# Attention and two expert layers: separate names for shared memory, merged loads, a fourth output buffer, a new table of order

## The chip, the cores and the metric

The kernel runs on one core of one Trainium2 chip. The metric is the device time of one execution in microseconds (us), the median of the runs shown. Three runs of the kernel before gave 1088.44, 1091.89 and 1093.85 us.

## The reference

Everything is float32. Attention has 4 batches of 8 heads, 576 positions and 64 channels; then come two pairs of dense layers (2304 tokens, 512 channels, 2048 hidden).

```python
scores = q @ k.T / 8                       # per batch and head, 576 x 576
keep   = scores >= max(scores, -1) - tau   # the others are set to -1e9
attn   = exp(scores - max); attn /= sum(attn) + 1e-9
x      = (attn @ v) laid out as (batch*seq, heads*64)
h = x @ w_in;  g = s * relu(h)**2 + b;  x = g @ w_out          # first layer pair
h = x @ w_in2; g = max(h,0) + alpha * min(h,0); out = g @ w_out2   # second pair
```

The weights arrive as 8-byte numbers and are turned into 4-byte ones on the chip.

## The kernel before

**How the order is made.** The kernel first lists about 6,800 tasks (`plan.add`): an engine, a time in us that the author gives, the buffers read and written, a rank. `Plan.run` (L696) then plays them in a simulated clock: whenever an engine is free it takes the ready task of the lowest rank whose buffers are open, and in that moment the task's instructions are issued. So the order in each engine's queue is fixed when the kernel is built; on the chip every engine works through its queue in that order and waits by semaphores where data is late. `MOVES` is a table that adds a number to the rank of task n; it is the order "written out". In the old planner a DMA costs SP 0.6 us and ends a fixed time later (`LAND` plus its kilobytes over 180, and `BUSY` added for some).

**Stages.** (1) The first batch's four head pairs ("whole" pairs): k and q are loaded, transposed by TensorE, scores are made (L1311) and reduced to a maximum (DVE L1321), exponentials are taken (ACT L1325), cut and summed (DVE L1327), transposed back by TensorE (`turned_e`, lines L848 and L850), copied out of PSUM by ACT (L1439) into tiles called exponentials here, and multiplied with v (L1451, a burst of 20 matmuls). (2) The other three batches do the same in a split form (L1471), and in the gaps the first layer pair ("MoE A", L1057 to L1059) runs on the columns that are done. (3) The rest of the first pair, from 480 us on. (4) The second pair, from 745 us on, which multiplies 2x2 blocks with seven products.

**Memory that the change touches.** `gt` is one large tile, placed at a fixed address under two names of type (`g32`/`gt`, L898). Its first part, ten slots, takes the first block's features (`g0_s`, written by ACT L1098 and POOL or DVE L1099). The rest is cut into slices that serve as exponentials of the first batch (`of_e`, L1145, shown in the profile as `gt`); later the whole tile holds other features.

**Transposes.** One transpose task turns 1 to 4 blocks; `flip` (L846) makes all but the last in a one-pass type (L848) and the last in plain float32 (L850).

**Outputs of stage 3.** Each block of 384 tokens gives four results; ACT (L1705) or DVE (L1714) writes each into a buffer of `yb_s` (three, L1605) and SP sends it to memory (L1707, L1717). `sm_s` (four buffers) holds block sums of the second pair's weights (`seven`, `weights`).

**Loads.** Each head pair's k, q and v come in one DMA per head (L1184, 128 KB each, rows of 64 channels), the last 64 positions in small ones (L1203, L1198). SP issues nearly all DMAs; the k and q splits go through SBUF copies (`hk`, `hq`, L1267 and L1271).

**Warm matmuls.** `warm` (L1407) is a 128x128 matmul whose result nobody reads: 12 at the start, a few behind the first pair's transposes and its first two scores (`FILL`, `FILLS`, `FILL1`).

Of the kernel before, what the change touches and what calls it, by code (L numbers as in the profile page):

```python
# [17 lines left out]
P = 128  # L18
# [13 lines left out]
FILL, FILL1 = 12, 3  # L32
# [5 lines left out]
BUSY = 180  # L38
# [620 lines left out]


class Task:
    __slots__ = ("ways", "engine", "fn", "bufs", "needs", "next", "tail", "port")


class Plan:
    HOP = 0.2
    SELF = {"ACT": 0.12, "DVE": 0.12, "POOL": 0.06}
    LAND = 2.0

    def __init__(self):  # L670
        self.tasks = []
# [1263 lines left out]
```

## Time and profile before

| what | value |
|---|---|
| median of 3 runs | 1091.89 us |
| the profiled execution | 1095.99 us |
| its span, first to last instruction | 1094.2 us |
| TensorE matmul busy (PE) | 1058.2 us (97%) |
| VectorE (DVE), ScalarE (ACT), GpSimd (POOL) busy | 873.7, 702.4, 351.3 us |
| mean granted TensorE clock | 0.988 |
| chain that ended last | PE 83%, DVE 5%, DMA 4%, ACT 4%, issue 2% |

The span leaves 1.8 us of the execution around it. The chain is followed back from the last instruction, at each step to what released it. Lines such as L1439 are those of the kernel before; the lines of a helper (L848, L1057) stand for all its callers.

### The profile page before, as it was taken

How to read it: one execution, taken by the hardware profiler on the slowest of the kernel's cores; microseconds unless marked ns; L12 is line 12 of the kernel's file. 1: busy time of each engine (PE TensorE's matmuls, PEld its weight loads, DVE VectorE, ACT ScalarE, POOL GpSimd, SP SyncE). 2: the span in 40 equal slices, each digit the busy share in tenths (PEclk: the TensorE clock that was granted, in tenths of full speed). 3: DMA queues.
4: the chain of work that ended last, by engine and by line, in shares of the span. 5: the costliest groups of instructions: out<-in, count | busy, mean ns of one | idle time of the engine just before them, and what ended most of it. 6: DMA issues, size and time to landing. Idle time of an engine off the chain costs nothing.

```text
span 1094.2 us, 21344 instructions
## 1 busy us (share of the span) xinstructions
PE 1058.2 (97%) x7074; PEld 1003.8 (92%) x7074; DVE 873.7 (80%) x1976; ACT 702.4 (64%) x1649; POOL 351.3 (32%) x494
## 2 busy tenths in 40 slices
PE   8788899999999999999989999999999999999998
PEld 7556699989898988999989999999999999999998
DVE  6787888987888888847766787578999999998882
ACT  5897878886987788753543264465656876655551
POOL 2576645653764467520000012020102334112110
PEclk9898999999999999999999999999999999999999
DMA  5763465565455554426475576337786564554531
GB/s 130 208 189 121 120 159 136 122 168 144 109 126 137 145 142 108 131 68 189 118 231 163 184 263 206 109 111 242 263 255 212 171 211 142 153 158 118 147 99 39
DMA packets 195183, 170.90 MB, mean 156 GB/s; under 512 B 73216, under 2 KB 173568, under 8 KB 195072
## 3 DMA queue, kind: packets, MB, share of 16 engines
q1 hardware_dynamic: 191888, 167.11, 53.6%
q10 hardware_dynamic: 3184, 2.43, 0.8%
q8 instruction: 55, 0.90, 0.3%
q14 instruction: 56, 0.46, 0.1%
HBM read 98.97 MB, written 49.28 MB: 135 GB/s over the span
## 4 chain that ended last, share of the span: by engine, by line
PE 83%; DVE 5%; DMA 4%; ACT 4%; issue 2%; POOL 1%; SPq 1%; DVEq 0%; ACTq 0%; POOLq 0%
PE bank L1057 13%; PE bank L1058 13%; PE bank L1059 13%; PE bank_b L1058 9%; PE bank_b L1057 9%; PE bank_b L1059 9%; PE sc L1311 7%; PE bank L1471 5%; PE bank L850 3%; PE bank L848 3%; DVE e L1327 1%; PE bank L1451 1%; DMA stg<-in_moe_w_in_dram 1%; DMA yf<-yb 1%; ACT e L1325 1%
## 5 line engine op out<-in xcount | busy, mean ns | idle before, releaser
L1327 DVE SCALAR_TENSOR_TENSOR e<-sc,mx,e 128x576 f32<-128x576 f32 x144 | 116.5, 812 | 16.8 <-ACT e L1325 13.1
L1321 DVE TENSOR_REDUCE mx<-sc 128x1 f32<-128x576 f32 x144 | 107.3, 751 | 19.5 <-PE sc L1311 18.1
L1325 ACT ACTIVATE e<-sc,mx 128x576 f32<-128x576 f32 x144 | 106.7, 744 | 9.5 <-DVE mx L1321 8.9
L850 PE MATMUL bank<-eyes_r,e 128*128 128x128 f32 (+1 forms) x320 | 89.5, 292 | 0.9 <-DVE e L1327 0.9
L1057 PE MATMUL bank<-xt,wa 128*128 128x480 f32 (+3 forms) x224 | 82.4, 368 | 0.8 <-ACT rest L1088 0.7
L1057 PE MATMUL bank<-gt0r,wa 128*128 128x384 f32 (+4 forms) x214 | 75.7, 354 | 2.1 <-ACT rest L1088 1.9
L1323 POOL TENSOR_SCALAR mx<-mx,tau_s 128x1 f32<-128x1 f32 x144 | 49.3, 343 | 83.6 <-DVE mx L1321 73.8
L1058 PE MATMUL bank<-xt,wa 128*128 128x480 f32 (+3 forms) x224 | 76.1, 340 | 0.0
L1059 PE MATMUL bank<-xt,wa 128*128 128x480 f32 (+3 forms) x224 | 76.0, 339 | 0.0
L1058 PE MATMUL bank<-gt0r,wa 128*128 128x384 f32 (+4 forms) x214 | 72.1, 337 | 0.0
L1059 PE MATMUL bank<-gt0r,wa 128*128 128x384 f32 (+4 forms) x214 | 72.0, 337 | 0.0
L1471 PE MATMUL bank<-gl,vt 128*128 128x256 f32 (+1 forms) x192 | 65.0, 340 | 0.2 <-POOL gl L1504 0.2
L1471 PE MATMUL bank<-gh,vt 128*128 128x256 f32 (+1 forms) x192 | 57.7, 301 | 0.0
L1035 POOL TENSOR_TENSOR wa<-stg,wa 128x256 fp32r<-128x256 f32 x9 | 7.1, 789 | 147.9 <-ACT wa L1034 147.9
L1509 DVE TENSOR_TENSOR gl<-bank,gh 128x256 fp32r<-128x256 f32 (+1 forms) x96 | 43.5, 453 | 12.7 <-ACT gh L1507 11.7
L1311 PE MATMUL sc<-k,q 128*128 128x288 f32 x200 | 47.5, 361 | 5.5 <-DMA k<-hk 2.9
L1507 ACT ACTIVATE gh<-bank 128x256 fp32r<-128x256 f32 (+1 forms) x96 | 39.7, 413 | 19.2 <-PE bank L850 18.1
L1519 POOL TENSOR_TENSOR gr<-gf,gh 64x256 fp32r<-64x256 f32 (+1 forms) x48 | 38.5, 801 | 40.8 <-DVE gl L1517 26.8
L850 PEld LDWEIGHTS bank<-eyes_r,e 128*128 128x128 f32 (+1 forms) x320 | 45.2, 141 | 5.3 <-DVE e L1327 1.3
L1057 PEld LDWEIGHTS bank<-xt,wa 128*128 128x128 f32 x224 | 43.5, 194 | 3.3 <-ACT rest L1088 1.6
L951 DVE SCALAR_TENSOR_TENSOR n<-stg,n 128x512 int32<-128x512 int32 x64 | 44.5, 696 | 1.0
L1504 POOL TENSOR_TENSOR gl<-gf,gh 128x256 fp32r<-128x256 f32 (+1 forms) x48 | 38.7, 806 | 20.2 <-ACT gh L1502 13.1
(697 smaller groups left out, 4140.9 us busy)
## 6 DMA issues: line engine op xcount, KB each, us to landing
stg<-in_moe_w_in_dram SPq DMA_DIRECT2D x32, 512.0 KB, 4.1
stg<-in_moe_w_out_dram SPq DMA_DIRECT2D x32, 512.0 KB, 3.9
gf<-gw SPq DMA_DIRECT2D x44, 192.0 KB, 3.0
gw<-gf SPq DMA_DIRECT2D x52, 128.0 KB, 2.9
q<-hq SPq DMA_DIRECT2D x24, 256.0 KB, 4.7
qo<-hq SPq DMA_DIRECT2D x24, 256.0 KB, 4.3
xt<-xs SPq DMA_DIRECT2D x14, 384.0 KB, 4.5
yf<-yb SPq DMA_DIRECT2D x24, 192.0 KB, 2.6
```

Of the source, the lines that this page charges most:

```text
L850: nc.tensor.transpose(to, part(x), one)
L951: add("DVE", dve(DM), lambda: nc.vector.scalar_tensor_tensor(ni(), word(0), 29, ni(), op0=ALU.logical_shift_right, op1=ALU.bitwise_or), (n ...
L1057: nc.tensor.matmul(o, lhsT=wl, rhs=mh, start=first, stop=False, skip_group_check=on_top)
L1058: nc.tensor.matmul(o, lhsT=wh, rhs=ml, start=False, stop=False, skip_group_check=on_top)
L1059: nc.tensor.matmul(o, lhsT=wh, rhs=mh, start=False, stop=last, skip_group_check=on_top)
L1311: nc.tensor.matmul(sp.t[:, x, :HS], lhsT=o[0][:, c], rhs=o[1][:, x * HS:(x + 1) * HS], start=n == 0, stop=n == len(passes) - 1)
L1321: add("DVE", dve(S), lambda sp=sp, mx=mx: nc.vector.tensor_reduce(mx.t[:, 0:1], sp.t[:, :, :HS], op=ALU.max, axis=AX.XY, negate=True), (sp ...
L1323: t2 = add("POOL", 0.26, lambda mx=mx: nc.gpsimd.tensor_scalar(mx.t[:, 1:2], mx.t[:, 0:1], -1.0, tau_s, op0=ALU.mult, op1=ALU.subtract), ( ...
L1325: add("ACT", act(S, 1), lambda sp=sp, mx=mx, e=e: nc.scalar.activation(halves(e.t), sp.t[:, :, :HS], AF.Exp, bias=mx.t[:, 0:1]), (sp, mx), ...
L1327: add("DVE", dve(S) + 0.065, lambda sp=sp, mx=mx, e=e, col=col, sums=sums: nc.vector.scalar_tensor_tensor(halves(e.t), sp.t[:, :, :HS], mx ...
L1471: nc.tensor.matmul(o.t[:, :n], lhsT=w.rearrange("p a b -> p (a b)"), rhs=m.t[:, :n], start=c == first and x == 0, stop=c == last and x == ...
L1509: add("DVE", dve(n), lambda hi=hi, lo=lo, gt=gt: nc.vector.tensor_tensor(lo.t[:, :n], gt.t[:, :n], f32(hi.t[:, :n]), op=ALU.subtract), (gt ...
```

## The change

- `gt` (later features), `g0` (the first block's features) and `ge0`, `ge1`, ... (the exponentials' slices) become separately named tensors at the same addresses as before.
- k and q of a head pair are loaded by one DMA each, with both heads; v too, and v's tile is laid out head by head, so that a head's four blocks of a position are one run of 1024 bytes.
- `yb_s` gets four buffers, `sm_s` three.
- Two warm matmuls follow every score of the first batch but those that had three (`FILL2`).
- The last block of a transpose task is also turned in the one-pass type where the planner saw the next TensorE task begin at once and both are transposes (`joined`). For this the planner issues a TensorE task only when the next one starts.
- The planner's costs are new: a DMA takes SP 0.5 us (0.65 or 1.0 for some), all DMAs share one simulated line, and transposes cost other times. `MOVES` is a new table for the new numbers of the tasks (68 more warm ones, 48 fewer loads).

```diff
-FILL, FILL1 = 12, 3
+FILL, FILL1, FILL2 = 12, 3, 2
...
 MOVES = {
-    0: -28.8, 1: -4.97, 2: 0.748, 3: 7.76, 4: -3.45, 5: -0.433, 6: 2.58, 7: -22.4, 8: -31.3, 9: -41.5, 10: -32.9, 11: -14.1, 12: -51.2, 13: -49.6,
...
+                        if e == "PE":
+                            joined = t.turn and freed == (now, True)
+                            us -= self.JOIN * joined
+                            release(joined)
+                            held_back, freed = t, (None, t.turn)
...
+                        end = now + us
+                        if t.load:
+                            end = line = max(line, end + self.SEND) + t.load
+                        at(end + t.tail, "end", t)
...
     def turned(k):
-        return 0.109 + (0.06 + 0.085 * (k - 2) if k > 1 else 0.0)
+        return 0.112 + 0.061 * (k - 1)
...
     def flip(to, x, part, i, n, one, one_r):
-        if i < n - 1:
+        if i < n - 1 or plan.joined:
             nc.tensor.transpose(to.bitcast(F32R), part(as_r[id(x)]), one_r)
...
-    g32 = placed(1, "gt", [P, (NA - 3) * 2 * TA])[0]
-    gt = as_r[id(g32)]
+    def at(name, n, dt, o):
+        return nc.alloc_sbuf_tensor_at(name, [P, n], dt, offset=o).ap()
+
+    ng, n0 = (NA - 3) * 2 * TA, NA * 2 * FIRST[0][1]
+    end[0] -= 4 * ng
+    gt, g0 = at("gt", ng, F32R, end[0]), at("g0", n0, F32R, end[0])
+    ge = [at(f"ge{i}", G2, F32, end[0] + 4 * (n0 + i * G2)) for i in range((ng - n0) // G2)]
...
-    def hwdge(fn, reads=(), writes=(), rank=None, kb=128, after=()):
-        return add("SP", 0.6, fn, reads, writes, after, rank, tail=Plan.LAND + kb / 180.0)
+    def carried(kb, part):
+        return 1.4 * kb * 1024 / part * (0.0083 + 0.0369e-3 * part) / 16
+
+    def hwdge(fn, reads=(), writes=(), rank=None, kb=192, after=(), part=1536, far=0.0, us=0.5):
+        return add("SP", us, fn, reads, writes, after, rank, tail=far, load=carried(kb, part))
...
-                for h in range(2):
-                    def load(t=t, src=src, h=h):
-                        nc.sync.dma_start(
-                            t.t[:, 0:NQ, h, :], src[b, h0 + h, 0:NQ * P, :].rearrange("(p c) d -> p c d", c=NQ))
-
-                    hwdge(load, (), (t,), base - 12 * STEP, 128 + BUSY * (p > 0))
+                if nm == "v":
+                    hwdge(lambda t=t, src=src: nc.sync.dma_start(
+                        t.t.rearrange("p c h d -> p (c h d)").rearrange("p (h x) -> p h x", h=2)[:, :, :NQ * D], src[b, h0:h0 + 2, 0:NQ * P, :].rearrange("h (p c) d -> p h (c d)", c=NQ)),
+                        (), (t,), base - 12 * STEP, 256, (), 1024, 0.4)
+                    continue
+                hwdge(lambda t=t, src=src: nc.sync.dma_start(
+                    t.t[:, :NQ], src[b, h0:h0 + 2, 0:NQ * P, :].rearrange("h (p c) d -> p c h d", c=NQ)),
+                    (), (t,), base - 12 * STEP, 256, (), 256, 0.4, 1.0)
...
-                        for _ in range(FILL1 if p == 0 and i < 2 else 0):
+                        for _ in range((FILL1 if p == 0 and i < 2 else FILL2) if base < NP * 4 * STEP else 0):
                             warm(LATER, plan.tasks[-1:])
...
-            for slots, n, name, shape in ((ya_s, 2, "yat", [P, TB]), (yb_s, 3, "yb", [P, TB]),
-                                          (sm_s, 4, "sm", [P, G1])):
+            for slots, n, name, shape in ((ya_s, 2, "yat", [P, TB]), (yb_s, 4, "yb", [P, TB]),
+                                          (sm_s, 3, "sm", [P, G1])):
```

## Rows read from the trace of the kernel before

**Rows 1.** Busy time by stage: window, length, each engine's busy us, PEclk, DMA

```profile
0.00:150.00 150.00, 129.53 (x841) 101.28 (x841) 117.48 (x256) 113.06 (x254) 85.36 (x127) 0.94 0.56 152
150.00:480.00 330.00, 323.48 (x2325) 300.99 (x2324) 276.36 (x645) 265.31 (x616) 185.46 (x278) 0.99 0.53 131
480.00:600.00 120.00, 115.64 (x636) 113.27 (x635) 75.50 (x139) 47.31 (x93) 1.89 (x2) 0.97 0.54 168
600.00:1075.00 475.00, 474.85 (x3159) 473.81 (x3158) 401.77 (x931) 275.94 (x687) 78.59 (x87) 1.00 0.58 177
```

**Rows 2.** PE's waits: waited for, us in total, times, longest

```profile
PE sc L1311 <- DVE e L1327: 4.3, 6, 2.4
PE bank L848 <- ACT e L1325: 3.4, 1, 3.4
PE sc L1311 <- DMA k<-hk: 2.9, 1, 2.9
PE bank_b L1057 <- ACT gt0r L1109: 2.6, 1, 2.6
PE bank L1057 <- ACT rest L1088: 2.6, 3, 1.9
```

**Rows 3.** Four stretches in which the granted clock was 0.50, columns as in Rows 1

```profile
33.40:40.20 6.80, 6.08 (x23) 4.71 (x24) 5.10 (x11) 4.39 (x11) 3.01 (x4) 0.50 0.65 199
101.60:108.40 6.80, 6.33 (x31) 5.57 (x30) 4.42 (x9) 4.72 (x11) 3.80 (x5) 0.50 0.40 125
139.20:142.60 3.40, 3.40 (x19) 3.40 (x18) 3.27 (x5) 2.71 (x8) 3.40 (x5) 0.50 0.37 117
569.30:576.10 6.80, 5.93 (x17) 5.53 (x18) 4.03 (x8) 1.73 (x4) 0.00 (x0) 0.50 0.71 218
```

**Rows 4.** A wait of ACT from 95 to 150 us, columns as in Rows 2

```profile
ACT gt0r L1098 <- PE bank L1451: 6.7, 3, 2.8
```

**Rows 5.** The chain from 95 to 150 us: start us, us, what

```profile
94.76 1.64 PE bank L1451 x12
...
96.48 0.42 ACT gt0r L1098
...
99.49 0.75 DVE e L1327 x2
```

**Rows 6.** A wait of ACT, in the whole span, columns as in Rows 2

```profile
ACT yb L1705 <- DMA yf<-yb: 4.6, 1, 4.6
```

**Rows 7.** The chain from 555 to 572 us

```profile
559.11 8.23 DMA yf<-yb
```

**Rows 8.** PE in order of time: start us, us, line, operands

```profile
14.56 0.30 PE L850 MATMUL bank<-eyes_r,nat 128*128 128x128 f32 x1
...
334.65 0.23 PE L848 MATMUL bank<-eyes_r,e4r 128*128 128x128 f32 x1
334.71 0.30 PE L850 MATMUL bank<-eyes_r,e 128*128 128x128 f32 x1
...
334.97 0.28 PE L1471 MATMUL bank<-gh,vt 128*128 128x256 f32 x1
335.09 0.23 PE L848 MATMUL bank<-eyes_r,e5r 128*128 128x128 f32 x1
...
479.50 0.30 PE L850 MATMUL bank<-eyes_r,e 128*128 128x128 f32 x1
```

**Rows 9.** DMA issues: operands, queue, count, KB each, median us to landing

```profile
stg<-in_moe_w_in_dram SPq DMA_DIRECT2D x32, 512.0 KB, 4.1
...
nat<-in_k_dram SPq DMA_DIRECT2D x32, 128.0 KB, 3.2
...
nat<-in_v_dram SPq DMA_DIRECT2D x24, 32.0 KB, 2.5
```

**Rows 10.** SP's time for one load's issue, L1184: min/median/max ns

```profile
L1184 SPq DMA_DIRECT2D nat<-in_k_dram x32: 543/604/1697, 0.7 to 413.2; - x32
```

**Rows 11.** Ten warm matmuls in a row at full clock, columns as in Rows 8

```profile
11.53 1.28 PE L1409 MATMUL bank<-eyes_r 128*128 128x128 f32 x10
```

More of the change, by code (lines that the diff above doesn't have):

```diff
@@ L37 @@
 AT_ONCE = 4
-BUSY = 180
 LAG = 2
@@ L661 @@
 class Task:
-    __slots__ = ("ways", "engine", "fn", "bufs", "needs", "next", "tail", "port")
+    __slots__ = ("ways", "engine", "fn", "bufs", "needs", "next", "tail", "port", "load", "turn")
 class Plan:
@@ L667, with add @@
     SELF = {"ACT": 0.12, "DVE": 0.12, "POOL": 0.06}
-    LAND = 2.0
+    SEND = 1.0
+    JOIN = 0.05
     def __init__(self):
-        self.tasks = []
-    def add(self, engine, us, fn, reads=(), writes=(), after=(), rank=None, tail=0.0, port=False):
+        self.tasks, self.joined = [], False
+    def add(self, engine, us, fn, reads=(), writes=(), after=(), rank=None, tail=0.0, port=False, load=0.0, turn=False):
         t = Task()
-        t.fn, t.next, t.tail, t.engine, t.port = fn, [], tail, None, port
+        t.fn, t.next, t.tail, t.engine, t.port, t.load, t.turn = fn, [], tail, None, port, load, turn
         n = len(self.tasks)
@@ L699, in run @@
         busy = dict.fromkeys(engines, False)
-        port = None
-        events, n, left = [], 0, len(self.tasks)
+        port = held_back = None
+        events, n, left, line, freed = [], 0, len(self.tasks), 0.0, (None, False)
         def at(time, kind, x):
@@ L710, in offer, with go, release @@
                 heapq.heappush(ready[e], (rank, t, us))
+        def go(t, e):
+            if len(t.ways) > 1:
+                t.fn(e)
+            else:
+                t.fn()
+        def release(joined):
+            nonlocal held_back
+            if held_back is not None:
+                self.joined = joined
+                go(held_back, "PE")
+                held_back = None
         for t in self.tasks:
@@ L735, in run @@
                         t.engine = e
-                        if len(t.ways) > 1:
-                            t.fn(e)
+                        if e == "PE":
[3 more added lines that the diff above has]
+                            held_back, freed = t, (None, t.turn)
                         else:
-                            t.fn()
+                            go(t, e)
                         busy[e] = True
                         at(now + us, "free", e)
-                        at(now + us + t.tail, "end", t)
+                        end = now + us
+                        if t.load:
+                            end = line = max(line, end + self.SEND) + t.load
+                        at(end + t.tail, "end", t)
                         break
@@ L752, in run @@
                     port = None
+                if x == "PE":
+                    freed = now, freed[1]
             elif kind == "end":
+                if x is held_back:
+                    release(False)
                 left -= 1
@@ L945, in mult @@
                 on(e).tensor_scalar(n32.t, f32(word(1)), REBIAS, None, op0=ALU.mult)
-        hwdge(load, (), (raw, *also), rank, 512, after)
+        hwdge(load, (), (raw, *also), rank, 512, after, 1024 if inner else 4096, 0.4)
         add([("DVE", 0.34, rank), ("ACT", act(DM, 0, True) + 0.04, rank)], 0, mult, (raw,), (n32,), port=True)
@@ L1043, in whole @@
         numbers(src, kind == "i", f, raw, n32, rank, after)
-        hwdge(lambda: nc.sync.dma_start(wf[kind][f * P:(f + 1) * P, :], n32.t), (n32,), (wf_d[kind][f],), rank, 262)
+        hwdge(lambda: nc.sync.dma_start(wf[kind][f * P:(f + 1) * P, :], n32.t), (n32,), (wf_d[kind][f],), rank, 256, (), 2048)
     def weights(kind, u, rank, after):
@@ L1050, in weights @@
             raw.t.rearrange("p (h n) -> p h n", h=2), wf[kind].rearrange("(h u p) n -> u p h n", h=2, p=P)[u]),
-            [wf_d[kind][u], wf_d[kind][u + NF // 2]], (raw,), rank, 524, after)
+            [wf_d[kind][u], wf_d[kind][u + NF // 2]], (raw,), rank, 512, after, 2048, 0.3)
         q = {f"{i + 1}{j + 1}": (raw, lambda o=(2 * i + j) * G1: raw.t[:, o:o + G1]) for i in range(2) for j in range(2)}
@@ L1068, in load_x @@
             t = hwdge(lambda x=x, c=c: nc.sync.dma_start(
-                f32(x.t[:, :, :n]), src[:, c * P:(c + 1) * P, c0:c0 + n].rearrange("a p t -> p a t")), bufs[c], (x,), rank, 1.024 * n, chain[0])
+                f32(x.t[:, :, :n]), src[:, c * P:(c + 1) * P, c0:c0 + n].rearrange("a p t -> p a t")), bufs[c], (x,), rank, n, chain[0], 4 * n, 0.6)
             xs.append(x)
@@ L1143, in attention @@
         v32, o = tiles(ep, NP, "v32", [P, NK, 2, D]), NS * P
-        f0 = NA * 2 * FIRST[0][1]
-        of_e = gf + sh + tiles(ep, 1, "gp", [P, G2]) + [g32[:, i:i + G2] for i in range(f0, g32.shape[1] - G2 + 1, G2)]
+        of_e = gf + sh + tiles(ep, 1, "gp", [P, G2]) + ge
         for t in of_e:
@@ L1165, in halves, with by_head @@
             return t.rearrange("p (a b) -> p a b", a=2)
+        def by_head(t):
+            return t.t.rearrange("p c h d -> p (c h d)").rearrange("p (h c d) -> p h c d", h=2, d=D)
         def half(h):
@@ L1181, in pair @@
                 t = nat[nm] = Buf(t=v32[p]) if nm == "v" and whole else Buf(nat_s)
-                for h in range(2):
-                    def load(t=t, src=src, h=h):
-                        nc.sync.dma_start(
-                            t.t[:, 0:NQ, h, :], src[b, h0 + h, 0:NQ * P, :].rearrange("(p c) d -> p c d", c=NQ))
-                    hwdge(load, (), (t,), base - 12 * STEP, 128 + BUSY * (p > 0))
+                if nm == "v":
[6 more added lines that the diff above has]
+                    (), (t,), base - 12 * STEP, 256, (), 256, 0.4, 1.0)
             if whole:
-                add("POOL", 0.2, lambda: nc.gpsimd.memset(nat["v"].t[TL:P, NQ], 0.0), (), (nat["v"],), rank=ready)
+                add("POOL", 0.2, lambda: nc.gpsimd.memset(by_head(nat["v"])[TL:P, :, NQ], 0.0), (), (nat["v"],), rank=ready)
             for nm, src in (("k", k), ("q", q), ("v", v)):
@@ L1227, in transpose @@
                                 flip(tr.t[:, i * P:(i + 1) * P], t.t, lambda x: x[:, c].rearrange("p h d -> p (h d)"), i, len(cs), ident, ident_r)
-                        add("PE", turned(1 if tail else NQ), transpose, (t,), (tr, hl), rank=ready)
+                        add("PE", turned(1 if tail else NQ), transpose, (t,), (tr, hl), rank=ready, turn=True)
                         for _ in range(FILLS[nm, tail] if p == 0 else 0):
@@ L1267, in pair @@
                             hwdge(lambda hl=hl, x=ks[h], a=a, i=i: nc.sync.dma_start(
-                                f32(x.t[half(i)[0]]), f32(hl.t[a, i, :])), (hl,), (ks[h],), ready, 147 + BUSY)
+                                f32(x.t[half(i)[0]]), f32(hl.t[a, i, :])), (hl,), (ks[h],), ready, 144, (), 2304, 1.1, 0.65)
                         continue
@@ L1271, in pair @@
                         hwdge(lambda hl=hl, x=qs[h], a=a, i=i: nc.sync.dma_start(
-                            f32(x.t[half(i)[0]]), f32(hl.t[a, :, :NQ * P])), (hl,), (qs[h],), ready, 262 + BUSY)
+                            f32(x.t[half(i)[0]]), f32(hl.t[a, :, :NQ * P])), (hl,), (qs[h],), ready, 256, (), 2048, 1.1, 0.65)
             nv = nat["v"]
@@ L1278, in pair @@
                 x = add("ACT", act(NK * 2 * D, 0, True), lambda: nc.scalar.activation(
-                    vp.t[:, :NK, 0:4:3, :], nv.t, AF.Copy), (nv,), (vp,), rank=ready)
+                    vp.t[:, :NK, 0:4:3, :], by_head(nv).rearrange("p h c d -> p c h d"), AF.Copy), (nv,), (vp,), rank=ready)
                 add("POOL", pool2(NK * 2 * D), lambda: nc.gpsimd.tensor_tensor(
-                    vp.t[:, :NK, 1:3, :], nv.t, f32(vp.t[:, :NK, 0:4:3, :]), op=ALU.subtract), (nv,), (vp,), after=(x,), rank=ready)
+                    vp.t[:, :NK, 1:3, :], by_head(nv).rearrange("p h c d -> p c h d"), f32(vp.t[:, :NK, 0:4:3, :]), op=ALU.subtract), (nv,), (vp,), after=(x,), rank=ready)
                 x = plan.tasks[-1]
                 for r, c in (slice(0, TL), NQ - 1), (slice(TL, P), NQ):
-                    hwdge(lambda r=r, c=c: nc.sync.dma_start(f32(vp.t[r, NK]), f32(vp.t[r, c])), (), (vp,), ready, 64 + BUSY, (x,))
+                    hwdge(lambda r=r, c=c: nc.sync.dma_start(f32(vp.t[r, NK]), f32(vp.t[r, c])), (), (vp,), ready, 64, (x,), 1024, 0.2, 0.65)
             for base, turns in stages:
@@ L1383, in spread @@
                     flip(pm.t[:, i * P:(i + 1) * P], rb.t, lambda x: x[:, i * P:(i + 1) * P], i, m, ident, ident_r)
-            add("PE", turned(m), spread, (rb,), (pm,), rank=rank)
+            add("PE", turned(m), spread, (rb,), (pm,), rank=rank, turn=True)
             add("DVE", dve(m * P), lambda: nc.vector.tensor_tensor(f32(z.t[:, c]), f32(z.t[:, c]), pm.t[:, :m * P], op=ALU.mult),
@@ L1404, in parts @@
                 hwdge(lambda x=x, i=i, c=c: nc.sync.dma_start(
-                    xs[i, (p % NP) * P:(p % NP + 1) * P, t0 + to.start:t0 + to.stop], x.t[:, c] if i == 0 else f32(x.t[:, c])), (x,), rows, rank, 0.512 * n)
+                    xs[i, (p % NP) * P:(p % NP + 1) * P, t0 + to.start:t0 + to.stop], x.t[:, c] if i == 0 else f32(x.t[:, c])), (x,), rows, rank, 0.5 * n, (), 4 * n)
         def warm(rank, after=()):
@@ L1437, in plain_group @@
                 add("PE", turned(2 + gi), lambda gt=gt, keys=keys, rows=rows: turned_e(gt, es, whole, h, gi, keys, rows),
-                    [es[i] for i in whole] + ([es[NQ]] if gi else []), (gt,), rank=rank)
+                    [es[i] for i in whole] + ([es[NQ]] if gi else []), (gt,), rank=rank, turn=True)
                 add("ACT", act(n), lambda f=f, gt=gt, rows=rows: nc.scalar.activation(
@@ L1487, in group @@
                 add("PE", turned(2 + gi), lambda gt=gt, keys=keys: turned_e(gt, es, whole, h, gi, keys, P),
-                    [es[i] for i in whole] + ([es[NQ]] if gi else []), (gt,), after=ahead(), rank=rank)
+                    [es[i] for i in whole] + ([es[NQ]] if gi else []), (gt,), after=ahead(), rank=rank, turn=True)
                 if c < NQ:
@@ L1710, in tile_kernel @@
                 hwdge(lambda p=p, d=d, c0=c0, n=n: nc.sync.dma_start(p.t[:, :n], ya[d * P:(d + 1) * P, c0:c0 + n]),
-                      [x[d] for x in within(c0, n, blocks_a, ya_d)], (p,), SOON, after=(sw,))
+                      [x[d] for x in within(c0, n, blocks_a, ya_d)], (p,), SOON, after=(sw,), far=0.1)
                 add("ACT", act(n, 1, True), lambda p=p, n=n, of_b=of_b: nc.scalar.activation(
@@ L1853, in tile_kernel @@
                                 gf2[f * P:(f + 2) * P, c0:c0 + P].rearrange("(a p) t -> p a t", p=P)),
-                                g_d[i][2 * l:2 * l + 2], (raw,), SOON, 131, ahead[0])
+                                g_d[i][2 * l:2 * l + 2], (raw,), SOON, 128, ahead[0], 512, 0.4)
                             gq[f"{b + 1}{h + 1}"] = raw, lambda raw=raw: raw.t[:, :G1]
@@ L1890, in store @@
                     for r, t0, step in rows(cs[b], P):
-                        add([("SP", 0.6, SOON), ("ACT", 0.6, LATER)], 0, lambda e, r0=r0, r=r, t0=t0, step=step: (
+                        add([("SP", 0.5, SOON), ("ACT", 0.5, LATER)], 0, lambda e, r0=r0, r=r, t0=t0, step=step: (
                             nc.sync if e == "SP" else nc.scalar).dma_start(
-                            out[t0:t0 + (r - 1) * step + 1:step, o:o + G1], x.t[r0:r0 + r, :G1]), (x,), (), tail=Plan.LAND + 0.7)
+                            out[t0:t0 + (r - 1) * step + 1:step, o:o + G1], x.t[r0:r0 + r, :G1]), (x,), (), tail=0.3, load=carried(r, 1024))
                         r0 += r
```

16 lines of the change are left out of this document (8 added, 8 removed), and 1141 rows, old and new, of the table MOVES.

## The prediction

> **What bounds the kernel now.** I read first the table by stage, then who PE waits for, then the stretches of halved clock, and last the chain at those places. The table [rows 1] is to be read as length minus PE busy: PE stands idle for 20.5 us in the first 150, for 6.5 us from there to 480, for 4.4 us to 600 and for 0.15 us in the 475 after that. So the second half is TensorE at its limit and no edit of order, buffers or loads helps it; what can be won lies ahead of 600 us, some 31 us of idle time, and in the clock, which was granted at 0.94, 0.99 and 0.97 in these three stages.
>
> The list of PE's waits [rows 2] shows the idle time is made of few long waits: 3.4, 2.9, 2.6, 2.4 and 1.9 us. Behind four of them stands a stretch at clock 0.50, which is 1.2 GHz instead of 2.4 [rows 3]. A halved stretch costs half of what PE was busy in it: 3.0, 3.2, 1.7 and 3.0 us in the order of the rows. So a long wait is paid twice, and this is the largest lever.
>
> **The change part by part.** All terms are set against the profiled execution, 1095.99 us.
>
> *Separate names: -7 us.* In the first batch ACT's writing of features (L1098) waited three times, 6.7 us, for the burst of PE that reads exponentials [rows 4]. The features and the exponentials are different slices of one tile, so no data passes between them: the wait comes from the tile's one name. ACT works in order, and behind the first wait stand the exponential and the weights' rounding; the chain runs from the burst over this ACT instruction to DVE at 99.5 [rows 5], for which PE waits 2.4 us; behind the third stands L1088, with 1.9 us [rows 2]. The two stretches at half clock that follow cost 3.2 + 1.7 us [rows 3]. Sum 9.2. With names apart the three waits go. What is late next: DVE is busy 117 and ACT 113 of the first 150 us [rows 1], and the scores need both in turn, so some wait of PE stays; I take 7. Bounds: 0, if waits are made by address and not by name, and 9.2. A loss is excluded, since the addresses and sizes stay.
>
> *Fourth yb buffer: -5.6 us.* The first block of stage 3 has four results for three buffers. Its first store took 8.2 us to land [rows 7] in a crowd of other transfers, the fourth result waited 4.6 us for its buffer with the whole of ACT behind it [rows 6], and PE waited 2.6 us for a feature of ACT's [rows 2]; then 6.8 us at half clock cost 3.0 [rows 3]. With four buffers the fourth result needs no store to land. Bounds 0 to -5.6; the late stores themselves then delay nothing, as their results are read only in the second pair. The buffer's place comes from `sm_s`, 4 to 3. These sums are made beside PE work in the later stages, where PE is idle 0.15 us and DVE has 73 of 475 us free [rows 1]: I take 0, with up to +3 (one long wait of [rows 2]) if weights come late.
>
> *Transposes: -3.5 us.* A one-pass transpose lets the next begin after 0.06 us (334.65 to 334.71). The plain last one and the product behind it take 0.26 us to 334.97, of which the next product of that size takes 0.12, so the last one costs 0.14, or 0.08 more [rows 8]. In PE's order of before 95 such last blocks have another transpose right behind them, the first at 14.56, the last at 479.50 [rows 8], 43 of them after 150 us, where PE is the limit: 43 x 0.08 = 3.4. Those ahead of 150 lie largely beside idle time. Bounds: 0, if the new order keeps none adjacent, and 95 x 0.08 = -7.6.
>
> *Merged loads: -2 us.* 96 issues become 48. At 0.60 us each [rows 10] this frees SP by 29 us if a merged issue costs the same and by nothing if it costs double. The transfer: 128 KB land in 3.2 us and 32 KB in 2.5, all in 256-byte runs, so 96 KB add 0.7 and a merged k or q should land after 4.1 us, where the pair of before ended 0.6 + 3.2 = 3.8 after the first issue: 0.3 later. v has runs of 1024 bytes now, as the 512 KB of weights with 4.1 us: 480 KB add 1.6, so v lands after 3.3, or 0.5 earlier [rows 9]. In PE's queue the first k stands behind the starting warm matmuls, which hide this; without that cover it costs 0.3. The stake is the 3.4 us wait at a transpose of a loaded tile [rows 2] and the half clock behind it, 3.0 [rows 3]: 6.4 if loads come in time. I take 2, since the weights' large loads share the queue and stay. Bounds -6.4 and +1.
>
> On this the Trainium skill has a rule that speaks against half of the edit: "DMA: Bandwidth & Descriptors", Specifications, gives 512 bytes as the least transfer for line rate. By it k and q, still in runs of 256 bytes, gain nothing in transfer by merging and only v does; by its figure of 27 GiB/s for each of 16 engines the merged v would move in an estimated 0.6 us beside the fixed latency, where the rows above give 0.75. The sum would be the same within 0.2 us, as both lie beside other work.
>
> *Warm matmuls: +2 us.* 34 scores x 2 = 68 more, at 0.11 us in a row [rows 11] 7.5 us of PE. They have the lowest rank, so the planner puts them where it sees PE idle; 20.5 us are idle there [rows 1]. But the order is fixed, and where the chip's idle time lies elsewhere they push the next score by 0.2. I take a quarter; bounds 0 and +7.5.
>
> *New order: 0.* Every queue is dealt anew, SP's and POOL's too. No row shows which waits it brings. Old ones, such as 2.9 us for a copy of k [rows 2] with half clock behind, may go; new ones of the same size may come. Bounds: all other idle time of 150 to 480 gone, -6.5 [rows 1], or five new waits of 2.9, +15.
>
> Sum: -7 - 5.6 - 3.5 - 2 + 2 = -16.1, so 1079.9 us. The profiled execution lies 4.1 us above the median of 1091.89, so against the runs I predict **1076 us**.
>
> **The rivals.**
>
> *A, slower: late copies in the new order.* The place is the k and q copies of the twelve later pairs on SP's queue. For: one of them already made PE wait 2.9 us, and a halved clock behind it costs about 1.7 as in [rows 3]; the merged k and q land later by 0.3 and the order was made for a simulated line. Price 4.6 for each. From four more such waits (18) the gain of 16.1 is eaten, from five it is slower by a measurable amount; with six, 27.6, the time is 1103. Against: SP has less to issue, and PE shows few such waits now.
>
> *B, the false wait gives way to a true one.* PE still waits for DVE and ACT in the first batch, and the clock still falls there. For: both engines are busy three quarters of that stage [rows 1]. Then the first term is 1 instead of 7: 1082. The same time comes out if separate names change no wait at all: 1083. Against: the longest waits of PE there end at instructions that stood behind the three false ones [rows 5].
>
> *C, the clock holds through the first batch.* The warm matmuls fill what is left. The three stretches of [rows 3] ahead of 150 us cost 7.9 together; of these my terms take about 5, so 3 more, and the warm ones then cost nothing (2), and the wait of 3.4 goes whole (another 3): 1068. Against: PE takes its queue in order, so warm matmuls stand ahead of or behind a late instruction and do not fill its wait.
> The trace shows this side: ahead of each halved stretch lies a wait of 1.9 to 3.4 us [rows 2, 3]. The Trainium skill, "TensorE: Matmul & The Clock Gate", HAM oscillation, says the same of waits for DMAs; by it rival C holds only if the waits themselves get shorter. The trace agrees.
>
> **How the numbers follow.** Forecast 0.56, with its own range 1068 to 1084; A 0.14, B 0.20, C 0.10. About 0.5%, 5.5 us, is what can be told from no change, so faster means below 1086.4 and slower above 1097.4. Of B a third falls above 1086.4, where another wait takes some of the rest too; of A four fifths is slower. Faster: 0.56 + 0.10 + 0.13 - 0.05 for an order that eats half of the gain = 0.74; same 0.15; slower 0.11. The range for eight in ten goes from C's less the 8 us that joined transposes and a better order could add, 1060, to 1091, B with the warm ones' full price of 7.5.
>
> **What would show it.** Right: no wait of ACT's feature instruction (L1098) on the burst; no wait of ACT on yf<-yb in stage 3 and clock 1.00 about 570 us; more one-pass transposes and fewer plain ones; PE idle in the first 150 us under 14 us with clock above 0.96; stage 600 to the end as long as before. Wrong: idle time of PE in 150 to 480 above 10 us with copies of k and q named as its cause (A); DVE named for PE's waits of the first batch at the same sum (B); a wait for `sm` or for weights ahead of the second pair.

## The result and the profile after

The changed kernel takes 1077.45 us (four runs, 1076.73 to 1078.27), the kernel before 1092.87 beside it. The ratio is 0.9862, 95% interval [0.9825, 0.9899], some 15 us faster; 1076 was predicted. The sum came out right, in part by luck: two of its terms were too large, one too small, and one edit does something that the prediction did not see.

The table by stage of the changed kernel, columns as in [rows 1], and then the four stretches that stood at half clock before [rows 3]:

```profile
0.00:150.00 150.00, 141.24 (x1030) 116.53 (x1031) 124.66 (x274) 115.99 (x266) 88.20 (x127) 1.00 0.59 158
150.00:480.00 330.00, 324.61 (x2327) 302.69 (x2325) 277.07 (x655) 259.40 (x600) 179.22 (x270) 1.00 0.53 130
480.00:600.00 120.00, 120.00 (x686) 120.00 (x686) 86.14 (x160) 49.22 (x94) 1.42 (x1) 1.00 0.63 193
600.00:1057.00 457.00, 456.54 (x3053) 455.36 (x3053) 386.38 (x896) 269.61 (x675) 88.23 (x96) 1.00 0.57 176
...
33.40:40.20 6.80, 6.14 (x45) 4.21 (x44) 5.78 (x12) 6.29 (x18) 4.96 (x5) 1.00 0.90 232
101.60:108.40 6.80, 6.67 (x54) 5.98 (x52) 6.76 (x14) 6.01 (x15) 4.78 (x5) 1.00 0.61 190
139.20:142.60 3.40, 3.40 (x31) 3.25 (x30) 3.00 (x7) 3.13 (x9) 0.76 (x3) 1.00 0.56 174
569.30:576.10 6.80, 6.80 (x41) 6.80 (x40) 4.81 (x10) 1.50 (x3) 0.00 (x0) 1.00 0.52 159
```

PE's idle time (length less PE busy) is 8.8 us in the first 150, where it was 20.5; 5.4 to 480, where it was 6.5; none to 600, where it was 4.4. The clock is 1.00 in every stage. PE's longest kinds of wait (waited for, us in total, times, longest), against [rows 2]:

```profile
PE sc L1394 <- DVE e L1410: 2.3, 3, 1.2
...
PE sc L1394 <- DMA q<-hq: 1.5, 1, 1.5
...
PE bank L1136 <- ACT rest L1676: 1.0, 2, 0.8
```

Behind the start no wait is above 1.5 us, where five stood between 1.9 and 3.4.

**Where the time went.** The time from PE's first matmul to the start of its last (the last matmul of L1136; of L1057 before) can be split in three: PE's idle time, the half of PE's busy time that a stretch at clock 0.50 costs, and the rest, which is the work at full clock. Worked out from each run's own trace, in us, one profiled execution each:

| kernel | work | idle | half clock | sum |
|---|---|---|---|---|
| before | 1045.1 | 29.9 | 12.6 | 1087.5 |
| changed | 1056.4 | 13.0 | 0.0 | 1069.4 |
| e1_old_names | 1045.3 | 25.2 | 8.2 | 1078.6 |
| e2_old_yb | 1045.1 | 29.5 | 9.1 | 1083.7 |
| e3_old_names_yb | 1044.0 | 24.2 | 4.2 | 1072.4 |
| e4_old_all | 1045.4 | 21.1 | 0.0 | 1066.5 |
| e6_new_nofill | 1044.5 | 19.8 | 0.0 | 1064.3 |
| e7_new_onename | 1057.0 | 19.9 | 5.5 | 1082.4 |
| e8_new_nojoin | 1057.3 | 13.9 | 0.0 | 1071.1 |
| e9_old_loads | 1046.6 | 26.9 | 4.8 | 1078.2 |
| e10_old_kq | 1045.6 | 30.0 | 6.6 | 1082.2 |
| e11_old_v | 1045.5 | 26.9 | 8.2 | 1080.5 |
| e12_old_join | 1046.3 | 33.0 | 9.8 | 1089.2 |

The change takes away 16.9 us of waiting and all 12.6 us of halved clock, and puts in 11.3 us of work, nearly all of it warm matmuls. Single executions differ by some us, most of all in the half clock; the timed medians decide.

### The profile page after: what moved, and what is told of

It is laid out like the page before. It is cut to its first block, busy times and chain, and to the rows that moved or that the text cites. A ratio compares the mean times of both kernels' runs of the same rounds, so it can differ in the third digit from the quotient of the medians.

```text
span 1076.0 us, 21525 instructions
## 1 busy us (share of the span) xinstructions
PE 1056.9 (98%) x7210; PEld 1008.9 (94%) x7210; DVE 876.9 (81%) x1989; ACT 695.0 (65%) x1636; POOL 357.1 (33%) x494
## 4 chain that ended last, share of the span: by engine, by line
PE 86%; DVE 6%; ACT 3%; DMA 3%; issue 2%; SPq 0%; POOL 0%; DVEq 0%; ACTq 0%; POOLq 0%
PE bank L1136 14%; PE bank L1137 13%; PE bank L1138 13%; PE bank_b L1137 8%; PE bank_b L1138 8%; PE bank_b L1136 8%; PE sc L1394 7%; PE bank L1554 5%; PE bank L919 4%; PE bank L921 3%; PE bank L1492 1%; PE bank L1534 1%; DVE e L1410 1%; DVE wb L1114 1%; DMA stg<-in_moe_w_in_dram 1%
## 5 line engine op out<-in xcount | busy, mean ns | idle before, releaser
L1136 PE MATMUL bank<-xt,wa 128*128 128x480 f32 (+3 forms) x235 | 87.0, 370 | 1.2 <-ACT rest L1676 0.8
L1137 PE MATMUL bank<-xt,wa 128*128 128x480 f32 (+3 forms) x235 | 79.1, 337 | 0.0
L1138 PE MATMUL bank<-xt,wa 128*128 128x480 f32 (+3 forms) x235 | 79.1, 336 | 0.0
L921 PE MATMUL bank<-eyes_r,e 128*128 128x128 f32 (+1 forms) x238 | 68.9, 291 | 0.5 <-DVE e L1410 0.5
L1136 PE MATMUL bank<-gt,wa 128*128 128x384 f32 (+3 forms) x173 | 62.2, 360 | 0.6 <-ACT gw L1868 0.3
L1137 PE MATMUL bank<-gt,wa 128*128 128x384 f32 (+3 forms) x173 | 59.7, 345 | 0.0
L1138 PE MATMUL bank<-gt,wa 128*128 128x384 f32 (+3 forms) x173 | 59.7, 345 | 0.0
L1101 POOL TENSOR_TENSOR sm<-stg 128x256 f32<-128x256 f32 x8 | 6.6, 835 | 135.3 <-DMA stg<-wfi 125.3
L1136 PEld LDWEIGHTS bank<-xt,wa 128*128 128x128 f32 x235 | 45.1, 192 | 3.8 <-ACT rest L1676 1.2
L1138 PEld LDWEIGHTS bank<-xt,wa 128*128 128x128 f32 x235 | 44.1, 188 | 2.4
L1137 PEld LDWEIGHTS bank<-xt,wa 128*128 128x128 f32 x235 | 44.5, 189 | 0.7
```

Source lines behind the costliest of these rows:

```text
L921: nc.tensor.transpose(to, part(x), one)
L1136: nc.tensor.matmul(o, lhsT=wl, rhs=mh, start=first, stop=False, skip_group_check=on_top)
L1137: nc.tensor.matmul(o, lhsT=wh, rhs=ml, start=False, stop=False, skip_group_check=on_top)
L1138: nc.tensor.matmul(o, lhsT=wh, rhs=mh, start=False, stop=last, skip_group_check=on_top)
```

## The experiments

Kernels named "old" keep the order of every queue of the kernel before (where loads are merged, one stands in the place of two); those named "new" keep the order of the changed kernel. Each ratio is to the kernel before, timed beside it in five rounds.

### Separate names alone

```diff
-    g32 = placed(1, "gt", [P, (NA - 3) * 2 * TA])[0]
-    gt = as_r[id(g32)]
...
+    gt, g0 = at("gt", ng, F32R, end[0]), at("g0", n0, F32R, end[0])
+    ge = [at(f"ge{i}", G2, F32, end[0] + 4 * (n0 + i * G2)) for i in range((ng - n0) // G2)]
```

> The kernel before with one edit, the separate names for features and exponentials; the order of every queue stays the old one. Theory W (the gain is long waits of PE and the half clock behind them, each removed by its own edit): ACT no longer waits for the burst, clock 1.00 from 95 to 145 us, 7 us less than before (1 to 9), about 1086. Rival O (the gain comes from the new order; on the old one the next wait takes the removed one's place): under 2 us less.

Measured: 1086.6 us, 0.9936 [0.9910, 0.9961], 7.0 us faster. The two stretches behind the false waits, columns as in [rows 3], and what is left of ACT's waits for the burst:

```profile
101.60:108.40 6.80, 5.96 (x46) 5.04 (x46) 5.02 (x13) 6.80 (x19) 4.28 (x5) 1.00 0.35 107
139.20:142.60 3.40, 3.40 (x32) 3.40 (x32) 3.15 (x10) 3.17 (x7) 0.69 (x2) 1.00 0.60 149
```
```profile
ACT z L1459 <- PE bank L1455: 1.7, 2, 1.4
```

The feature instruction no longer waits for the burst [rows 4]; what does wait is `z`, which reads the burst's result and must. PE runs at 1.00 where it ran at 0.50. So the wait came from the tensors as they were laid out before.

It did not come from one name, as the prediction has it. `placed` gives the memory two named tensors, both over the whole of it: the feature writes `gt0r` [rows 4], and the burst reads `gt0`, which the profile prints as `gt` (rows under e12_old_join, below). The wait goes from one to the other, so it is set by tensors that overlap in memory, each taken as a whole. The new tensors end it because those of features and of exponentials no longer overlap.

### One memory for both again, in the changed kernel

```diff
-    gt, g0 = at("gt", ng, F32R, end[0]), at("g0", n0, F32R, end[0])
-    ge = [at(f"ge{i}", G2, F32, end[0] + 4 * (n0 + i * G2)) for i in range((ng - n0) // G2)]
+    gt, g32 = at("gt", ng, F32R, end[0]), at("g32", ng, F32, end[0])
+    g0, ge = gt[:, :n0], [g32[:, o:o + G2] for o in range(n0, ng - G2 + 1, G2)]
```

> The changed kernel with features and exponentials again in one named memory, the order the new one. Theory W: the waits of ACT on the burst come back, with PE idle and half clock behind, 7 us more, about 1084.5. Rival O (the new order places features and bursts so that the name does not matter): 1078 to 1079.

Here too the two sides have different names, `gt` and `g32`, over the same memory. Measured: 1090.74 us, 0.9976 [0.9961, 0.9992]; the changed kernel, run beside it, had 1077.37. The loss is 13 us, twice what was expected. PE's waits, one of these bursts (it reads `g32`, printed as `g`), and the two half-clock stretches:

```profile
PE bank L1534 <- DVE gt L1178: 5.3, 2, 3.4
PE bank L1534 <- POOL gt L1178: 2.9, 1, 2.9
```
```profile
101.14 1.86 PE L1534 MATMUL bank<-g,v 128*64 128x320 f32 x5 [3.37 <-DVE gt L1178]
```
```profile
99.39:106.21 6.82, 5.07 (x20) 2.19 (x20) 3.02 (x7) 2.40 (x5) 1.35 (x2) 0.50 0.26 77
140.35:147.17 6.82, 5.98 (x22) 2.64 (x23) 0.47 (x2) 0.33 (x1) 0.72 (x1) 0.50 0.01 3
```

Here the false wait has the other direction: before, the feature waited for the burst; now the burst, on PE itself, waits for the feature. Why it turned is argued under e12_old_join, below.

### The fourth output buffer

Its memory is borrowed in these runs: for eight uses, the first two blocks of stage 3, a tile that is used only later (`of[2]`) serves as the fourth. `sm_s` keeps its four buffers.

```diff
+            yb_s.free = Rota(late["yb"], of[2], 8)
```

> The kernel before with one edit, a fourth memory for the outputs of the first two blocks of stage 3 (borrowed from a tile that is idle then), the order of every queue as before. Theory W: no wait of ACT on yf<-yb, clock 1.00 about 570 us, 5.6 us less (up to 7), about 1087. Rival O: the late stores stall something else, under 2 us less.

Measured: 1092.11 us, 0.9982 [0.9957, 1.0008], so 2 us less, with an interval from -4.7 to +0.9 that holds zero.

> Both edits of the two runs before on the old order. Theory W: they lie in different stages and add, 12 to 13 us less, about 1080. Rival O: under 4 us less.

Measured, with separate names too: 1082.27 us, 0.9906 [0.9876, 0.9937], 4.3 us under e1_old_names by the medians. The stretch about 570 us in e2_old_yb, against [rows 3], and PE's only listed wait from 540 to 600 us:

```profile
569.30:576.10 6.80, 6.20 (x36) 5.89 (x35) 5.54 (x10) 2.75 (x6) 0.00 (x0) 1.00 0.73 215
```
```profile
PE bank_b L1075 <- DVE gt0r L1127: 1.1, 2, 0.6
```

The mechanism is right: the wait for a store [rows 6], the 2.6 us on PE and the halved clock are gone. The size was not: from the last split product to the 500th product of the dense layers behind it (580 us in the kernel before) the six kernels with three buffers in the old order (before, e1, e9, e10, e11, e12) lost 7.3, 5.3, 4.4, 4.4, 6.4 and 5.9 us to idle time and half clock together, mean 5.6; the three with four (e2, e3, e4) lost 2.0, 3.1 and 1.3, mean 2.1. The difference is 3.5. The execution on which the prediction was made had the largest loss of the six, and some loss remains with four buffers.

### Names, buffer, joined transposes and merged loads, in the old order

The edit has these four parts of the diff. The queues keep the old order: `FILL2`, the planner's new costs and the new `MOVES` are left out. The fourth buffer is borrowed as above, so `sm_s` keeps four.

> The kernel before with names, the fourth output memory, joined transposes and merged loads, the old order in every queue (a merged load stands where the first of the two stood). No warm matmuls are added. Theory W: 12.6 for the first two, 3.5 for the transposes and 2 for the loads, 18 us less, about 1075, so the new order and the added warm ones together are worth nothing or a small loss. Rival O: 8 us or more are missing, 1084 or above.

Measured: 1077.14 us, 0.9853 [0.9822, 0.9883]. For comparison the changed kernel itself, timed in the same way:

> The changed kernel as it is, for the same chip as the three that follow: 1077.5, ratio to before 0.986.

Measured: 1077.37 us, 0.9855 [0.9833, 0.9876]. In e4_old_all no stretch at half clock is left before the last 2 us (columns as in [rows 1]):

```profile
0.00:150.00 150.00, 134.41 (x953) 107.01 (x954) 126.31 (x285) 122.43 (x278) 91.06 (x135) 1.00 0.64 169
...
480.00:600.00 120.00, 118.72 (x677) 118.00 (x676) 87.14 (x157) 50.32 (x98) 1.02 (x1) 1.00 0.59 184
```

So the new table of order and the 136 new records of warm matmuls together gain nothing that this timing tells: the other edits make the whole gain. By themselves names with the buffer (e3_old_names_yb) and the loads (e9_old_loads, below) gave 10.3 and 3.1 us of these 16.1; the other 2.7 lie within the intervals, and no run says where they come from.

### The changed kernel without the new warm matmuls

```diff
-                            warm(LATER, plan.tasks[-1:])
+                            warm(LATER, plan.tasks[-1:], not (p == 0 and i < 2))
...
-            add("PE", pe(P, 2), lambda: nc.tensor.matmul(w.t[:, :P], lhsT=ident, rhs=ident, start=True, stop=True), (), (w,), after, rank)
+            add("PE", pe(P, 2), lambda: None if silent else nc.tensor.matmul(w.t[:, :P], lhsT=ident, rhs=ident, start=True, stop=True), (), (w,), after, rank)
```

> The changed kernel without its 68 added warm matmuls (they only write a bank that nobody reads); the order of all else stays. Theory W with the prediction's price: they cost 2 us, so 1075.5, with the clock still 1.00 but for short stretches. Rival C (they hold the clock): without them the clock falls to 0.50 once or more in the first 150 us and the time is 1080 or above. Rival P (each is two records of 0.11 us on PE's path): 6 to 12 us less, 1066 to 1071.

The order of all else is held. Measured: 1075.83 us, 0.9835 [0.9811, 0.9859], beside 0.9855 [0.9833, 0.9876] with them: 1.5 to 2.2 us less, and the intervals overlap. The first 150 us without them, and PE's longest waits:

```profile
0.00:150.00 150.00, 133.20 (x927) 105.00 (x928) 126.48 (x284) 118.03 (x272) 90.93 (x130) 1.00 0.61 163
```
```profile
PE sc L1394 <- DVE e L1410: 3.0, 4, 1.2
PE bank L919 <- ACT sh L1522: 2.3, 4, 1.1
```

PE idles 16.8 us here, only 3 less than in e9_old_loads (19.8), where the clock fell at 98 us behind a wait of 2.4; here it is 1.00. In these two the halved clock goes with the single long wait, not with the sum: behind the start none is above 1.4 us here. So the clock does not need the warm matmuls (rival C); that it holds by the absence of long waits is what the traces suggest. This is the fastest kernel measured, though not shown to beat the changed one.

### The changed kernel with plain last transposes

```diff
-        if i < n - 1 or plan.joined:
+        if i < n - 1:
```

> The changed kernel with the last block of every transpose task in plain float32 again (101 more of them), the order the new one. Theory W: 101 at 0.06 to 0.08 us, half of them where PE is the limit, 3.5 us more, about 1081. Rival (the time is hidden): no change, 1077.5.

Measured: 1077.47 us, 0.9844 [0.9818, 0.9869]; no difference to the changed kernel. All its work at full clock is 1057.3 us against 1056.4 and 1056.1 in two executions of the changed kernel: 0.01 us for each of the 101 joined blocks, at most.

### Joined transposes alone, in the old order

The planner's issuing is part of this edit: a TensorE task is issued when the next one starts, since only then is it known whether they join. 85 last blocks join here (plain transposes fall from 388 to 303), where the prediction counted 95.

> The kernel before with only the joined transposes (the last block of a transpose task also in one pass where another transpose follows at once), old order. By the prediction's term the time falls by 3.5 us, ratio 0.997; by what e8_new_nojoin measured (undoing the joins in the changed kernel cost nothing that timing tells, 1.4 to 2 us by the end of PE's last matmul) it falls by 0 to 2 us, ratio 0.998 to 1.000. The 95 or so joined blocks should each leave PE 0.06 to 0.08 us earlier where PE is the limit.

Measured: 1097.03 us, 1.0060 [1.0038, 1.0081]: **slower** by 6.5 us, which no theory had. PE's waits from 60 to 160 us:

```profile
PE bank L1469 <- POOL gt0r L1117: 7.8, 3, 3.8
```

Now the same burst and the same feature in both kernels, in order of time (start us, us, engine, line, operands). Before:

```profile
80.89 0.43 PE L1451 MATMUL bank<-gt,v 128*64 128x320 f32 x1
...
81.36 0.42 ACT L1098 ACTIVATE gt0r<-rest 128x256 fp32r<-128x256 f32 x1 [0.55 <-PE bank L1451]
81.86 0.73 POOL L1099 TENSOR_TENSOR gt0r<-rest,gt0r 128x256 fp32r<-128x256 f32 x1 [2.00 <-ACT gt0r L1098]
```

With joined transposes:

```profile
82.48 0.46 ACT L1116 ACTIVATE gt0r<-rest 128x256 fp32r<-128x256 f32 x1
83.02 0.76 POOL L1117 TENSOR_TENSOR gt0r<-rest,gt0r 128x256 fp32r<-128x256 f32 x1 [1.16 <-ACT gt0r L1116]
...
83.84 0.79 PE L1469 MATMUL bank<-gt,v 128*64 128x320 f32 x1 [3.41 <-POOL gt0r L1117]
```

The order of the two has turned, although each engine's queue has the same order in both. Before, the burst (ending 81.3) comes first and the feature waits; here the feature comes first and the burst starts 0.06 us after POOL's part of it. Between tasks whose tensors overlap, the one issued first in the program goes first. Holding a burst back in the planner issues it behind features that the planner started meanwhile, and so the false wait moves from ACT to PE, where it costs more: 3.41 us here, 3.75 at 116 and half clock behind. With separate tensors there is nothing to turn, which fits that e4_old_all does not have this loss, and that the shared memory costs 7 us in the old kernel and 13 in the changed one. Holding back without joining was not run by itself; that it, and not the type of the transposes, turns the order is argued from the code and from e7_new_onename, where the same direction appears.

The joined blocks themselves give nearly nothing. A stretch with PE at its limit and two joined blocks between, first before, then joined:

```profile
28.91 1.14 PE L1311 MATMUL sc<-k,q 128*128 128x288 f32 x4
...
30.45 0.27 PE L850 MATMUL bank<-eyes_r,e 128*64 128x128 f32 x1
```
```profile
29.59 1.14 PE L1329 MATMUL sc<-k,q 128*128 128x288 f32 x4
...
31.08 0.27 PE L868 MATMUL bank<-eyes_r,e 128*64 128x128 f32 x1
```

From the first start to the last: 1.54 us and 1.49 us, 0.025 for each block. In the split batches, from the last burst to the last split product, the work at full clock is 336.6 us in both old-order kernels with joined blocks and 336.0 to 336.5 in seven without: no gain.

### Merged loads in the old order

```diff
                 for h in range(2):
-                    def load(t=t, src=src, h=h):
-                        nc.sync.dma_start(
-                            t.t[:, 0:NQ, h, :], src[b, h0 + h, 0:NQ * P, :].rearrange("(p c) d -> p c d", c=NQ))
+                    def load(t=t, src=src, h=h, v=nm == "v"):
+                        if h:
+                            return
...
+                            nc.sync.dma_start(t.t[:, :NQ], src[b, h0:h0 + 2, 0:NQ * P, :].rearrange("h (p c) d -> p c h d", c=NQ))
```

All of k, q and v:

> The kernel before with only the loads changed: k, q and v of a head pair in one DMA each, v laid out by head; every queue keeps the old order. Open is which of joined transposes and merged loads made the 5 us between the runs e3_old_names_yb and e4_old_all. Theory 'loads': the 3.4 us wait of a transpose for a loaded tile and the half-clock stretch at 33 us (3.0 us) go, so the time is 3 to 6 us under the kernel before, ratio 0.9945 to 0.9972, and the trace has no stretch at 0.50 before 95 us. Rival 'joins': the wait at 30 us stays or only moves, the ratio is 0.998 to 1.0005.

Only k and q, and only v:

> Of the loads only k and q merged (rows of 256 bytes kept), v as before, old order. If what matters is SP's time (one issue of about 0.6 us in place of two), this gives most of what e9_old_loads gives: ratio 0.995 to 0.998, the wait at 30 us gone. If what matters is the transfer of v in runs of 1024 bytes, it gives nothing or loses: ratio 0.999 to 1.001, with the wait at 30 us still there.

> Of the loads only v merged and laid out by head (runs of 1024 bytes), k and q as before, old order. By SP's time: 8 to 12 of the 48 issues saved, ratio 0.998 to 1.000, and the wait at 30 us stays. By transfer: ratio 0.995 to 0.998 and the wait at 30 us goes.

Measured: all 1088.08 us, 0.9972 [0.9955, 0.9988]; k and q 1090.53, 0.9973 [0.9951, 0.9994]; v 1088.36, 0.9967 [0.9947, 0.9987]. All are faster, by 3 us; which half does it is **not settled** by these times, as the intervals cover each other. The wait for a loaded tile at 31 us, first before (the 3.4 us of [rows 2]), then in the three in that order:

```profile
34.12 0.59 PE L848 MATMUL bank<-eyes_r,nat0r 128*128 128x128 f32 x3 [3.41 <-ACT e L1325]
```
```profile
32.38 0.42 PE L848 MATMUL bank<-eyes_r,nat0r 128*128 128x128 f32 x3 [0.96 <-DMA nat<-in_q_dram]
```
```profile
34.11 0.59 PE L848 MATMUL bank<-eyes_r,nat0r 128*128 128x128 f32 x3 [2.60 <-ACT e L1328]
```
```profile
PE bank L848 <- DMA nat<-in_q_dram: 1.9, 1, 1.9
```

Two of these rows name ACT's `e`, which ended within 0.05 us of the load; in all four the transpose starts 0.09 to 0.14 us after the last part of the tile has landed, which fits a wait for the load. With v merged that part lands 1.6 us (v alone) and 1.7 us (all) sooner than before, at 32.36 and 32.25 us against 33.99. With k and q alone it lands at 33.97, and PE waits less only because it comes to this place 0.8 us later: the first transpose of all waits for the merged k, whose tile is complete at 6.69 us where it was at 5.05. First before, then with k and q merged:

```profile
5.92 0.52 PE L848 MATMUL bank<-eyes_r,nat0r 128*128 128x128 f32 x3
```
```profile
6.82 0.43 PE L848 MATMUL bank<-eyes_r,nat0r 128*128 128x128 f32 x3 [0.56 <-DMA nat<-in_k_dram]
```

So at this wait it is v's half that helps. Both together leave 0.96, and of the three kernels only that one keeps its clock through the stretch at 33 us [rows 3]:

```profile
33.40:40.20 6.80, 5.92 (x40) 3.50 (x38) 6.08 (x14) 6.03 (x16) 5.42 (x6) 1.00 0.82 237
```

What the loads cost, from e4_old_all (SP's time for one issue, min/median/max ns, against [rows 10]) and from the changed kernel (KB, median us to landing, against [rows 9]):

```profile
L1232 SPq DMA_DIRECT2D nat<-in_k_dram x16: 610/649/1019, 0.7 to 397.7; - x16
```
```profile
nat<-in_k_dram SPq DMA_DIRECT2D x16, 256.0 KB, 4.0
nat<-in_q_dram SPq DMA_DIRECT2D x16, 256.0 KB, 4.3
nat<-in_v_dram SPq DMA_DIRECT2D x12, 256.0 KB, 3.5
```

A merged issue costs SP what one half did, so the pair's second 0.6 us is saved; k and q land after 4.0 and 4.3 us (estimated 4.1), v after 3.5 (3.3). v with its 1024-byte runs lands sooner than k at the same size, in line with the rule of 512 bytes in the Trainium skill, "DMA: Bandwidth & Descriptors", Specifications, that the prediction weighed. k and q land no sooner than the pair of before (3.8 after its first issue), and yet e10_old_kq is faster, by an interval that leaves out 1; so their gain, if it is theirs, is not one of landing time.

## Why the prediction was right, point by point

| step | predicted | measured |
|---|---|---|
| separate names | -7 | -7.0 (e1_old_names); 13 in the changed kernel |
| fourth buffer | -5.6 | -2.0 alone, -4.3 beside names; 3.5 from the traces |
| joined transposes | -3.5 | 0 in work; +6.5 alone, by a turned false wait |
| merged loads | -2 | -3.1 |
| warm matmuls | +2 | +1.5 to +2.2 |
| new order | 0 | e6_new_nofill against e4_old_all, 0.9835 and 0.9853 of the kernel before: none that is told |

*Names, right in size, and wrong in what makes the wait.* The chain from the three waits through DVE to the halved clock held in both directions, and "what is late next" was small, as assumed. That "the wait comes from the tile's one name" did not hold: in the kernel before and in e7_new_onename the two sides have two names, and wait because their tensors overlap. The step also missed that the false wait's direction hangs on the order of issue: the change's own planner would have made it worse, so the separate tensors are worth more in the kernel that they came with.

*Fourth buffer, mis-sized.* The price was read from one execution, which was the worst of six, and the term let nothing remain where 2.1 us remain.

*Transposes, wrong.* The step that failed is "the last one costs 0.14, or 0.08 more" [rows 8]: it took the distance between starts of overlapping records for PE's time. Between two points with the same work PE saves 0.025 us a block, and in whole stages nothing.

*Loads, too small.* The stake of 6.4 was right, and the old order took about half of it. That the starting warm matmuls "hide this" did not hold in the old order: with k merged PE's first transpose starts 0.8 to 0.9 us later (e9_old_loads, e10_old_kq).

*Warm matmuls, right by two errors.* A warm matmul shows as two records (50 before, 186 after, for 68 more), and the ten records of [rows 11] are five of them, so the full price was not 7.5 but, at 0.11 a record, 15:

```profile
L1492 PE MATMUL bank<-eyes_r x186: 270/275/582, 1.6 to 136.5; 128*128 128x128 f32 x186
```

The work with them is 11.8 us more (1056.3 against 1044.5, the mean of two executions), 0.17 each; 6.5 of that stood in idle time (19.8 to 13.3). The profiles say 5 us of net cost, the timing 1.5 to 2.2: the profiled execution of e6_new_nofill took 1072.74, under its median of 1075.83.

*The half clock.* Not four but five of the long waits had a halved stretch behind them: the one behind the 2.9 us for a copy of k, 3.4 us long, is not among [rows 3] and cost 1.7. The prediction names it under the new order, at 0; it went, and in e4_old_all it went without the new order.

*The signs named beforehand.* ACT's feature instruction waits for no burst and ACT for no yf<-yb in stage 3, the clock is 1.00 about 570 us, the records of plain transposes fall from 388 to 287, and PE idles 8.8 us in the first 150 at clock 1.00. These are as forecast. Of the signs of being wrong none is in the trace of the changed kernel: PE idles 5.4 us from 150 to 480, its scores wait 2.3 us for DVE's `e` where it was 4.3 [rows 2], and it has 0.5 us of idle time from 600 to 1057.

*The rivals.* A (late copies): the waits for q and k copies are 1.5 and 0.5 us, no clock falls behind them. B (a true wait takes over): PE still waits for DVE and ACT in the first batch, but behind the start never above 1.2 us. C (warm matmuls hold the clock): the clock holds through the first batch, but it does so without them. The buffer gave 1.3 to 3.6 less than priced and the joins 3.5 less; the loads gave 1.1 more and the order up to 2 more. Together that is 2 to 6 us, inside the interval of the ratio (some 8 us wide), so the sum alone would not have shown it.

## What to carry to other kernels

Slices of tensors that overlap in memory may be ordered against each other though no data passes, and a second name over the same memory does not help. The direction is that of issue, so an edit of the planner can turn a wait from a side engine onto the busiest one. Give each use a tensor of its own, over its slice alone, before touching the order. Price a wait from several executions, and a saving per instruction between two points with equal work, not from the starts of overlapping records. Look for single long waits, not for the sum of idle time.

## What was not expected of the hardware

The halved stretch (1.2 GHz) is not a fixed price of a wait. Runs are named here by their first part.

- The wait of PE for `rest` near 130 to 135 us took 1.86 to 1.87 us in the kernel before and in e2, e9, e10 and e11: a stretch at 0.50 lasting 3.41 us followed in four of them, none in e9.
- The wait for the k copy between 231 and 252 us was followed by 3.41 us where it took 2.5 to 3.5 (before, e1, e3, e9, e10), by 6.83 where it took 4.3 (e2), and by none at 2.60 (e12), at 1.98 (e4) and at 1.74 (e11).
- The wait in stage 3 was followed by 6.83 us in the kernel before (2.59) and e11 (1.77), by 3.41 in e1 (1.77), e9, e10 and e12 (1.85 to 2.10).

The same wait of 1.77 us in e1 and e11, then the place behind the 2.60 us in e12 (columns as in [rows 3]):

```profile
562.44:565.84 3.40, 3.40 (x13) 3.40 (x12) 1.75 (x3) 0.52 (x1) 0.00 (x0) 0.50 0.88 280
562.04:568.84 6.80, 6.10 (x19) 5.76 (x19) 3.55 (x7) 1.20 (x3) 0.00 (x0) 0.50 0.72 232
251.73:258.53 6.80, 6.79 (x50) 6.67 (x50) 5.38 (x12) 4.34 (x11) 2.86 (x5) 1.00 0.21 44
```

So no length of wait parts the two cases. In the kernels whose longest wait behind the start is 1.3 to 2.0 us (changed, e4, e6, e8) the clock does not fall before the last 5 us. This fits that the kernel before spreads over 11 us in 30 runs (1088.26 to 1099.71) and the changed one over 2.8 in the six of e5_after (1075.84 to 1078.59). The clock goes along with it: the fastest of the thirty had a mean granted clock of 0.995 and the slowest 0.985, the six of e5_after 0.999 to 1.000. The Trainium skill, "TensorE: Matmul & The Clock Gate", HAM oscillation, ties the fall to waits too, those for DMAs; the traces agree that it follows waits, for ACT and DVE as well, and add how unevenly it comes.
